# The first group of a fused attention and MLP kernel: another order of loads, casts and row blocks

## The chip, the cores and the metric

The kernel runs on one core of a Trainium2 chip. The metric is device time in microseconds (us). Before the change the median of 10 runs is 310.26 us (309.45 to 311.67). The engines are TensorE (PE: matrix products and, with an identity matrix, transposes), VectorE (DVE), ScalarE (ACT: exp, GELU, copies and casts), GpSimd (POOL: element work[...]) and SyncE (SP), whose queue issues the DMAs.

## The reference

The reference is an attention over pooled keys and values, followed by an MLP with the tanh form of GELU. B = 8 batches, H = 8 heads, S = 576 positions, D = 64, so 4608 rows of 512 columns enter the MLP, whose inner width is 2048. All inputs and the output are float32.

```python
k_p = k.reshape(B, H, Sp, pool, D).mean(axis=3)     # pool = 8, Sp = 72
v_p = v.reshape(B, H, Sp, pool, D).mean(axis=3)
scores = scale * np.matmul(q, k_p.transpose(0, 1, 3, 2))
scores = scores - np.max(scores, axis=-1, keepdims=True)
attn = np.exp(scores)
attn = attn / (np.sum(attn, axis=-1, keepdims=True) + 1e-09)
attn_out = np.matmul(attn, v_p)
x = np.ascontiguousarray(attn_out.transpose(0, 2, 1, 3)).reshape(B * S, H * D)
h = x @ w_in
g = 0.5 * h * (1.0 + np.tanh(c * (h + 0.044715 * h * h * h)))
out = g @ w_out
```

## The kernel before

**Groups.** The rows go through in nine groups of 512. Group g (0 to 7) holds the first 512 positions of batch g; group R (index 8) holds the last 64 positions of all eight batches. The order is 0 to 6, R, 7. A group has four row blocks j of 128 rows.

**Attention of a group.** K and V arrive in one tile `kv` (`load_main`, `load_half`). `pool` sums eight positions in three DVE additions (lines 128 to 130) into `kvb`; for two of V's parts of batch 0 `pool_v_pe` does it with 16 PE products instead (line 136). K is doubled (`dup_k`), transposed and copied by `k_spread` into `kbd`, in which each pair of heads has its own 64 partitions, the others being zero. `spread_v` multiplies V on POOL with a mask (line 148) into `vbd`. q is loaded, cast to bf16 (`cast_q`) and transposed to `qT`. For each row block, `scores` makes four products (line 208; for group R eight products, line 213, half of the rows each, since each 64 rows belong to another batch), `exps` takes the exponential on ACT from PSUM (line 221), `norm` sums, inverts and multiplies (lines 228, 230 and 231) into `eb`, and `eb` is transposed to `eT`: on PE (`e_transpose_pe`, line 240) for group 0, by a transposing DMA (`e_transpose_dma`, line 244) for the others. `values` multiplies with `vbd` (line 267; R line 273) and ACT copies the result to `xT`. Group 0 does this in halves of 256 rows (`values_half`, line 256).

**MLP of a group.** `hidden` (line 297) makes 16 column blocks fo of the first product, each from four partial products ko, and ACT applies GELU (line 299) into `gT`. `output` (line 302) makes the second product, 64 products of 512 columns, and `finish` copies and stores.

**The order.** It is written out by hand. While PE does the products of one group, functions of the next group's attention are called at numbered steps: `at(hooks, s, f, ...)` calls f just before the s-th product. An engine works through its instructions in the order of these calls. Every table (`preload_act_table_set`) is loaded on ACT where the call stands.

**The first group** is apart. Before it there is only a prologue (lines 362 to 460): loads, warm-up products on PE (`warm_up`, line 411), the attention of group 0, and casts of the weights. The weights w_in and w_out come as float32 in four chunks of 1 MB each and are cast to bf16 once (`cast_w_in`, `cast_w_out`, through the helper `copy`, lines 78 and 80). w_in chunk c holds the column blocks fo = 4c to 4c + 3; w_out chunk c holds the same fo of the second product. `mlp_first` goes through (half of the rows, chunk) pairs: steps 0 to 127 are products of the first kind with 256 columns, steps 128 on are products of the second kind, for fo 0 to 11 with the four row blocks inside, and then fo 12 to 15 for each row block.

**Loads and buffers.** All loads stand in SP's queue in program order: K, half tiles, half of q, V and the other half of q of batch 0; the four chunks of w_in; K, half tiles, q and V of batch 1; the four chunks of w_out. The tiles `kv`, `w_in_s` and `w_out_s` share three buffers (pool `kvp`), so batch 1's K waits until batch 0's V was read, and the w_out tiles wait for the casts of w_in. SP also holds the transposing DMAs and the stores.

Of the kernel before, what the change touches and what calls it, by code (L numbers as in the profile page):

```python
# [8 lines left out]
F32 = mybir.dt.float32  # L9
BF16 = mybir.dt.bfloat16  # L10
ALU = mybir.AluOpType
# [8 lines left out]
def kernel(  # L20
# [55 lines left out]
    def copy(eng, out, in_):  # L76
        if eng is nc.scalar:
            eng.copy(out=out, in_=in_)  # L78
        else:
            eng.tensor_copy(out=out, in_=in_)  # L80
# [121 lines left out]
    def scores(g, j):  # L202
        sc = psum.tile([128, 2, MAIN], F32, name="sc", tag="sc", bufs=2)
        qT = st[g]["qT"]
        for pr in range(HP):
            o = sc[:, pr // 2, 2 * Sp * (pr % 2):2 * Sp * (pr % 2) + 2 * Sp]
            if g < B:
                nc.tensor.matmul(out=o, lhsT=qT[:, j, pr, :], rhs=kbd[:, g, pr].rearrange("d hh s -> d (hh s)"),  # L208
                                 start=True, stop=True)
            else:  # L210
                for half in range(2):
                    p0 = 64 * half
                    nc.tensor.matmul(out=o[p0:p0 + 64], lhsT=qT[:, j, pr, p0:p0 + 64],
                                     rhs=kbd[:, 2 * j + half, pr].rearrange("d hh s -> d (hh s)"),
                                     start=True, stop=True)
        st[g][("sc", j)] = sc
# [8 lines left out]
    def norm(g, j, eng):  # L225
        e = st[g][("e", j)]
        den = work.tile([128, H], F32, name="den")
        nc.vector.reduce_sum(out=den, in_=e, axis=AX.X)  # L228
        r = work.tile([128, H], F32, name="r")
        nc.vector.reciprocal(out=r, in_=den)  # L230
        eng.tensor_tensor(out=eb[:, j, 128 * 5 - W:].rearrange("p (h s) -> p h s", s=Sp), in0=e,  # L231
                          in1=r.unsqueeze(2).to_broadcast([128, H, Sp]), op=ALU.mult)
# [16 lines left out]
    def values_half(g, half, engs):  # L249

        for x in range(2):
            xo = psum.tile([128, 2, 256], F32, name="xo", tag="mm", bufs=4)
            for i in range(2):
                pr = 2 * x + i
                for y, (c, n) in enumerate(PARTS[pr]):
                    nc.tensor.matmul(out=xo[:, i, :], lhsT=vbd[:, g, n, :],
                                     rhs=st[g]["eT"][:, 2 * half:2 * half + 2, c, :], start=(y == 0), stop=(y == 1))
            copy(engs[x], st[g]["xT"][:, 2 * x:2 * x + 2, 256 * half:256 * half + 256], xo)
# [77 lines left out]
    def mlp_first(g, hooks):  # L336
# [3 lines left out]
        for half, c in [(0, 0), (0, 1), (0, 2), (0, 3), (1, 0), (1, 1), (1, 2), (1, 3)]:  # L340
            for fo in range(4 * c, 4 * c + 4):
                hidden(g, fo, 256 * half, 256 * half + 256, hook, s)
                s += 4
# [24 lines left out]
    load_q(0, 0, 2, nc.sync)  # L368
    load_main(0, "v", 0, 2, nc.sync)
    load_main(0, "v", 2, 4, nc.sync)  # L370
    load_q(0, 2, 4, nc.sync)
# [10 lines left out]
    def cast_w_in(c, eng):  # L382
        o = 512 * c
        copy(eng, w_in_b[:, :, o:o + 512], w_in_s[c // 2][:, :, 512 * (c % 2):512 * (c % 2) + 512])
# [46 lines left out]
    warm_up(14, "mm")  # L431
    cast_q(0, 0, 2, nc.vector)
    q_transpose_pe(0, 0, nc.vector, "mm")
    q_transpose_pe(0, 1, nc.scalar, "mm")
    warm_up(6, "sc")
    for j in range(2):
        scores(0, j)
        exps(0, j)
    pool(0, 5, 7)
    spread_v(0, nc.gpsimd, (0,))  # L440
    pool_v_pe(0, 7, 9, nc.scalar)
    spread_v(0, nc.gpsimd, (1, 2))
    warm_up(8, "mm")
    norm(0, 0, nc.vector)
    norm(0, 1, nc.vector)
    cast_q(0, 2, 4, nc.scalar)
    e_transpose_pe(0, 0, nc.scalar)
    q_transpose_pe(0, 2, nc.scalar, "mm")
    q_transpose_pe(0, 3, nc.scalar, "mm")
    for j in range(2, 4):  # L450
        scores(0, j)
        exps(0, j)
    nc.scalar.preload_act_table_set(GELU_SET)
    e_transpose_pe(0, 1, nc.vector)
    cast_w_in(0, nc.vector)
    values_half(0, 0, [nc.scalar, nc.vector])
    norm(0, 2, nc.gpsimd)
    cast_w_in(1, nc.vector)
    norm(0, 3, nc.vector)
    cast_w_in(2, nc.gpsimd)  # L460
# [4 lines left out]
    def first_v():  # L465
        cast_w_in(3, nc.vector)
        values_half(0, 1, [nc.scalar, nc.vector])
# [8 lines left out]
    load_main(1, "v", 0, 4, nc.sync)  # L476
    for c in range(4):
        w_out_load(c)
# [20 lines left out]
    at(hooks, 16, first_t, 2)  # L499
    at(hooks, 32, first_t, 3)  # L500
    at(hooks, 42, first_v)
    at(hooks, 66, pool, 1, 0, 4)
    at(hooks, 66, dup_k, 1, 0, 4)
    at(hooks, 66, pool, 1, 4, 5)
    at(hooks, 66, dup_k, 1, 4, 5)
    at(hooks, 80, cast_q, 1, 0, 2, nc.vector)
    at(hooks, 80, cast_q, 1, 2, 4, nc.vector)
# [3 lines left out]
    at(hooks, 96, k_spread, 1, [nc.vector, nc.vector])  # L511
    for j in range(4):
        at(hooks, 104 + 6 * j, q_transpose_pe, 1, j, nc.vector, "sc")
    at(hooks, 122, eT_tile, 1)
    at(hooks, 122, pool, 1, 5, 9)
    at(hooks, 122, spread_v, 1, nc.gpsimd)
    at(hooks, 122, cast_w_out, 0, nc.gpsimd)
    at(hooks, 122, cast_w_out, 1, nc.gpsimd)
# [6 lines left out]
    at(hooks, 141, cast_w_out, 3, nc.scalar)  # L525
# [3 lines left out]
    tail_of_attention(hooks, 1, 186)  # L529
# [75 lines left out]
```

## Time and profile before

| | us |
|---|---|
| median of 10 runs | 310.26 |
| profiled execution | 311.05 |
| its span | 309.3 |
| PE busy (95% of the span) | 294.3 |
| ACT busy (51%) | 158.8 |
| DVE busy (47%) | 145.2 |
| POOL busy (18%) | 56.3 |
| first product with w_in starts | 20.17 |
| first product with w_out starts | 45.27 |
| values of batch 1 start | 61.34 |

The profile is one execution on the chip, and its times start at the beginning of the span. A busy PE isn't PE at its peak[...]. Idle time of another engine costs nothing unless PE waits for that engine in the end. An instruction's wait is put down to what came last.

### The profile page before, as it was taken

Reading aid. Unit: us, or ns where it says so; the run is one execution under the profiler, and the core shown is the slowest. Engines: PE = TensorE matmul, PEld = TensorE weight load, DVE = VectorE, ACT = ScalarE, POOL = GpSimd, SP = SyncE. Lnnn points to the kernel's source line nnn. Section 1 sums busy time; section 2 is a strip of 40 time slices with the busy share of each in tenths; the row PEclk is TensorE's granted clock in tenths of the full one; section 3 lists DMA queues with packets and bytes.
Section 4 is the critical chain, followed back from the end, with each engine's and each line's share of the span. In section 5 each row is a group of like instructions: output and inputs, shape, how many; then the busy total and the mean of one; then the engine's idle time right before and its main releaser. Section 6 shows DMA issues by size and latency. Waiting matters only on the chain.

```text
span 309.3 us, 4581 instructions
## 1 busy us (share of the span) xinstructions
PE 294.3 (95%) x1738; PEld 153.8 (50%) x1738; DVE 145.2 (47%) x237; ACT 158.8 (51%) x242; POOL 56.3 (18%) x71
## 2 busy tenths in 40 slices
PE   8969919999999999999999999999999999999996
PEld 8748904444544454445444544444444544544444
DVE  6877774162551755176435734483448200720012
ACT  1477734376806671667257626752674257625600
POOL 3323071022130312032203310340024000100000
PEclk9999986999999999999999999999999999999999
DMA  8999982899169937993899289437983810261012
GB/s 243 359 387 342 386 277 43 244 353 222 28 147 287 281 97 138 316 259 85 140 317 275 60 151 316 125 75 162 323 193 77 167 47 2 53 135 36 0 64 72
DMA packets 73221, 56.32 MB, mean 182 GB/s; under 512 B 45808, under 2 KB 55408, under 8 KB 73200
## 3 DMA queue, kind: packets, MB, share of 16 engines
q1 hardware_dynamic: 73056, 55.98, 65.6%
q8 instruction: 13, 0.21, 0.3%
q14 instruction: 8, 0.07, 0.1%
q10 hardware_dynamic: 144, 0.07, 0.1%
HBM read 36.70 MB, written 9.44 MB: 149 GB/s over the span
## 4 chain that ended last, share of the span: by engine, by line
PE 86%; DMA 4%; DVE 3%; POOL 2%; SPq 1%; ACT 1%; issue 1%; DVEq 0%; POOLq 0%
PE mm L297 40%; PE mm L302 37%; PE xo L267 4%; DMA q_sb<-in_q_dram 3%; PE sc L208 2%; DMA eT<-eb 1%; PE mm L330 1%; DVE den L228 1%; POOL w_out_b L80 1%; POOL vbd L148 1%; POOL eb L231 1%; SPq L98 1%; PE xo L273 1%; DVE kv L128 0%; DVE w_in_b L80 0%
## 5 line engine op out<-in xcount | busy, mean ns | idle before, releaser
L302 PE MATMUL mm<-w_out_b,gT 128*128 128x512 bf16 x560 | 131.1, 384 | 6.3 <-POOL w_out_b L80 6.3
L297 PE MATMUL mm<-xT,w_in_b 128*128 128x512 bf16 (+1 forms) x640 | 127.6, 358 | 0.8 <-ACT xT L78 0.8
L299 ACT ACTIVATE gT<-mm 128x512 bf16<-128x512 f32 (+1 forms) x160 | 88.7, 555 | 48.1 <-PE mm L297 46.8
L297 PEld LDWEIGHTS <-w_in_b 128*128 128x128 bf16 x640 | 62.3, 98 | 62.8 <-issue 0.6
L302 PEld LDWEIGHTS <-gT 128*128 128x128 bf16 x560 | 54.1, 99 | 66.6 <-issue 8.7
L80 DVE COPY osb<-mm 128x512 f32<-128x512 f32 (+2 forms) x37 | 24.4, 659 | 70.1 <-PE mm L302 68.0
L228 DVE TENSOR_REDUCE den<-e 128x8 f32<-128x576 f32 x36 | 26.5, 737 | 46.3 <-ACT e L221 46.3
L78 ACT CAST xT<-xo 128x1024 bf16<-128x1024 f32 (+1 forms) x18 | 16.6, 967 | 57.4 <-PE xo L267 48.9
L148 POOL TENSOR_TENSOR vbd<-kvb,vmask 128x256 bf16<-128x256 bf16 (+2 forms) x40 | 20.3, 531 | 118.7 <-DVE kvb L130 118.4
L128 DVE TENSOR_TENSOR kv<-kv 128x1024 f32<-128x1024 f32 (+3 forms) x19 | 22.0, 1160 | 24.1 <-DMA kv<-in_v_dram 22.7
L221 ACT ACTIVATE e<-sc 128x576 f32<-128x576 f32 x36 | 22.3, 649 | 17.9 <-PE sc L208 11.7
L231 DVE TENSOR_TENSOR eb<-e,r 128x576 bf16<-128x576 f32 x28 | 27.5, 982 | 1.2 <-DVE r L230 0.2
L231 POOL TENSOR_TENSOR eb<-e,r 128x576 bf16<-128x576 f32 x8 | 10.0, 1251 | 79.9 <-ACT e L221 46.0
L80 POOL CAST q_b<-q_sb 128x2048 bf16<-128x2048 f32 x6 | 14.0, 2332 | 13.6 <-DMA q_sb<-in_q_dram 13.6
L208 PEld LDWEIGHTS <-qT 128*128 128x128 bf16 x128 | 10.4, 101 | 8.0 <-issue 1.1
L208 PE MATMUL sc<-kbd,qT 128*128 128x144 bf16 x128 | 13.6, 232 | 0.5 <-ACT qT L78 0.5
L267 PE MATMUL xo<-eT,vbd 128*128 128x512 bf16 x56 | 13.2, 379 | 0.0
L129 DVE TENSOR_TENSOR kv<-kv 128x512 f32<-128x512 f32 (+3 forms) x19 | 12.3, 649 | 0.6
L411 PE MATMUL warm<-identb 128*128 128x128 bf16 x116 | 9.9, 258 | 1.4 <-POOL vmask L399 1.4
L490 ACT ACT_TABLE_LOAD x8 | 10.3, 1283 | 0.1
L411 PEld LDWEIGHTS <-identb 128*128 128x128 bf16 x116 | 9.1, 120 | 1.5 <-POOL vmask L399 1.4
L80 DVE COPY kbd<-kTd 64x288 bf16<-64x288 bf16 x12 | 5.3, 440 | 8.5 <-DMA kTd<-kvb 8.4
(54 smaller groups left out, 102.6 us busy)
## 6 DMA issues: line engine op xcount, KB each, us to landing
out_dram<-osb SPq DMA_DIRECT2D x31, 256.0 KB, 6.4
kv<-in_k_dram SPq DMA_DIRECT2D x7, 1024.0 KB, 6.8
q_sb<-in_q_dram SPq DMA_DIRECT2D x7, 1024.0 KB, 5.8
kv<-in_v_dram SPq DMA_DIRECT2D x7, 1024.0 KB, 9.4
w_in_s<-in_moe_w_in_dram SPq DMA_DIRECT2D x4, 1024.0 KB, 12.5
w_out_s<-in_moe_w_out_dram SPq DMA_DIRECT2D x4, 1024.0 KB, 13.9
out_dram<-osb SPq DMA_DIRECT2D x9, 128.0 KB, 2.3
kv<-in_k_dram SPq DMA_DIRECT2D x2, 512.0 KB, 4.0
```

Source lines behind the costliest of these rows:

```text
L80: eng.tensor_copy(out=out, in_=in_)
L128: add(out=t[:, :, 0:4, :], in0=t[:, :, 0:4, :], in1=t[:, :, 4:8, :], op=ALU.add)
L148: eng.tensor_tensor(out=vbd[p0:128, b, n0:n1, :].rearrange("p (c r) (hh d) -> p c (r hh) d", c=max(m, 1), d=D), in0=kvb[p0:128, 4 + c0:4 + ...
L208: nc.tensor.matmul(out=o, lhsT=qT[:, j, pr, :], rhs=kbd[:, g, pr].rearrange("d hh s -> d (hh s)"), start=True, stop=True)
L221: nc.scalar.activation(out=e.rearrange("p (x h) s -> p x (h s)", x=2), in_=sc[:, :, 0:4 * Sp], func=ACT.Exp, scale=1.0 / 64.0)
L228: nc.vector.reduce_sum(out=den, in_=e, axis=AX.X)
L231: eng.tensor_tensor(out=eb[:, j, 128 * 5 - W:].rearrange("p (h s) -> p h s", s=Sp), in0=e, in1=r.unsqueeze(2).to_broadcast([128, H, Sp]), ...
L267: nc.tensor.matmul(out=xo[:, i, :], lhsT=vbd[:, g, n, :], rhs=eT[:, :, c, :], start=(x == 0), stop=(x == 1))
L297: nc.tensor.matmul(out=hp[:, 0:c1 - c0], lhsT=w_in_b[:, ko, fo * 128:(fo + 1) * 128], rhs=st[g]["xT"][:, ko, c0:c1], start=(ko == 0), stop ...
L299: nc.scalar.activation(out=gT[:, fo, c0:c1], in_=hp[:, 0:c1 - c0], func=ACT.Gelu_apprx_tanh)
L302: nc.tensor.matmul(out=o, lhsT=gT[:, fo, r * 128:(r + 1) * 128], rhs=w_out_b[:, fo, :], start=(fo == 0), stop=(fo == FO - 1))
L411: nc.tensor.matmul(out=warm[:, 0:128], lhsT=identb, rhs=identb, start=True, stop=True)
```

## The change

The change has these parts.

- q of batch 0 comes in one load, ahead of V. Its cast is split over DVE (block 0), ACT (block 1) and POOL (blocks 2 and 3). All four blocks are transposed, scored and exponentiated one after the other, and ACT's table for GELU is loaded after the last exp; then V is pooled and spread, and blocks 0 and 1 are normalised.
- w_in chunk 0 is cast half by POOL and half by ACT, chunks 1 and 3 by POOL, chunk 2 by DVE inside `first_v`, which is now called at step 32. Blocks 2 and 3 are both normalised on DVE and transposed at steps 12 and 24. Both copies of the first half's values are on ACT.
- `mlp_first` takes the second half of the rows through chunk 0 before the first half through chunk 3.
- Batch 1: K, the half tiles and q are loaded first, then w_out chunks 0 and 1, half of V, chunk 2, the other half of V, chunk 3. V is pooled and spread at step 160 (before: 122). q is cast at step 100 (before: 80). w_out chunk 0 is cast by DVE at step 124 (before: POOL), chunk 3 by ACT at step 156.
- Group R: each of a row block's eight score products becomes two, with only the 64 partitions of one head, 64 rows and 72 columns; even heads go to one PSUM bank and odd heads to the other, and `norm` puts them back in order when it writes `eb`.

```diff
-            else:
-                for half in range(2):
-                    p0 = 64 * half
-                    nc.tensor.matmul(out=o[p0:p0 + 64], lhsT=qT[:, j, pr, p0:p0 + 64],
-                                     rhs=kbd[:, 2 * j + half, pr].rearrange("d hh s -> d (hh s)"),
-                                     start=True, stop=True)
+            for hh in range(2):
+                for p0 in (0, 64):
+                    h0 = 64 * hh
+                    nc.tensor.matmul(out=sc[p0:p0 + 64, hh, Sp * pr:Sp * pr + Sp],
+                                     lhsT=qT[h0:h0 + 64, j, pr, p0:p0 + 64],
+                                     rhs=kbd[h0:h0 + 64, 2 * j + p0 // 64, pr, hh], start=True, stop=True)
...
+            eng.tensor_tensor(out=o.rearrange("p (pr hh s) -> p hh pr s", hh=2, s=Sp),
+                              in0=e.rearrange("p (hh pr) s -> p hh pr s", hh=2),
...
-        for half, c in [(0, 0), (0, 1), (0, 2), (0, 3), (1, 0), (1, 1), (1, 2), (1, 3)]:
+        for half, c in [(0, 0), (0, 1), (0, 2), (1, 0), (0, 3), (1, 1), (1, 2), (1, 3)]:
...
-    load_q(0, 0, 2, nc.sync)
+    load_q(0, 0, 4, nc.sync)
     load_main(0, "v", 0, 2, nc.sync)
     load_main(0, "v", 2, 4, nc.sync)
-    load_q(0, 2, 4, nc.sync)
...
-    warm_up(14, "mm")
-    cast_q(0, 0, 2, nc.vector)
+    warm_up(12, "mm")
+    cast_q(0, 0, 1, nc.vector)
+    cast_q(0, 1, 2, nc.scalar)
+    cast_q(0, 2, 4, nc.gpsimd)
     q_transpose_pe(0, 0, nc.vector, "mm")
     q_transpose_pe(0, 1, nc.scalar, "mm")
-    warm_up(6, "sc")
...
+    q_transpose_pe(0, 2, nc.vector, "mm")
+    scores(0, 0)
+    exps(0, 0)
+    scores(0, 1)
     q_transpose_pe(0, 3, nc.scalar, "mm")
-    for j in range(2, 4):
+    exps(0, 1)
+    for j in (2, 3):
         scores(0, j)
         exps(0, j)
     nc.scalar.preload_act_table_set(GELU_SET)
+    pool(0, 5, 7)
+    spread_v(0, nc.gpsimd, (0,))
+    spread_v(0, nc.gpsimd, (1,))
+    pool_v_pe(0, 7, 9, nc.scalar)
+    spread_v(0, nc.gpsimd, (2,))
+    norm(0, 0, nc.vector)
+    norm(0, 1, nc.vector)
+    cast_w_in(0, nc.gpsimd, 0, 2)
+    e_transpose_pe(0, 0, nc.scalar)
+    cast_w_in(0, nc.scalar, 2, 4)
+    warm_up(8, "mm")
     e_transpose_pe(0, 1, nc.vector)
-    cast_w_in(0, nc.vector)
-    values_half(0, 0, [nc.scalar, nc.vector])
-    norm(0, 2, nc.gpsimd)
-    cast_w_in(1, nc.vector)
+    values_half(0, 0, 0, nc.scalar)
+    values_half(0, 0, 1, nc.scalar)
+    norm(0, 2, nc.vector)
+    cast_w_in(1, nc.gpsimd)
     norm(0, 3, nc.vector)
-    cast_w_in(2, nc.gpsimd)
+    cast_w_in(3, nc.gpsimd)
...
     def first_v():
-        cast_w_in(3, nc.vector)
-        values_half(0, 1, [nc.scalar, nc.vector])
+        values_half(0, 1, 0, nc.vector)
+        values_half(0, 1, 1, nc.scalar)
+        cast_w_in(2, nc.vector)
...
     load_q(1, 0, 4, nc.sync)
-    load_main(1, "v", 0, 4, nc.sync)
-    for c in range(4):
-        w_out_load(c)
+    w_out_load(0)
+    w_out_load(1)
+    load_main(1, "v", 0, 2, nc.sync)
+    w_out_load(2)
+    load_main(1, "v", 2, 4, nc.sync)
+    w_out_load(3)
...
-    at(hooks, 16, first_t, 2)
-    at(hooks, 32, first_t, 3)
-    at(hooks, 42, first_v)
+    at(hooks, 12, first_t, 2)
+    at(hooks, 24, first_t, 3)
+    at(hooks, 32, first_v)
...
-    at(hooks, 80, cast_q, 1, 0, 2, nc.vector)
-    at(hooks, 80, cast_q, 1, 2, 4, nc.vector)
...
+    at(hooks, 100, cast_q, 1, 0, 2, nc.vector)
+    at(hooks, 100, cast_q, 1, 2, 4, nc.vector)
     for j in range(4):
-        at(hooks, 104 + 6 * j, q_transpose_pe, 1, j, nc.vector, "sc")
-    at(hooks, 122, eT_tile, 1)
-    at(hooks, 122, pool, 1, 5, 9)
-    at(hooks, 122, spread_v, 1, nc.gpsimd)
-    at(hooks, 122, cast_w_out, 0, nc.gpsimd)
-    at(hooks, 122, cast_w_out, 1, nc.gpsimd)
+        at(hooks, 111 + 4 * j, q_transpose_pe, 1, j, nc.vector, "sc")
+    at(hooks, 124, eT_tile, 1)
+    at(hooks, 124, cast_w_out, 0, nc.vector)
+    at(hooks, 124, cast_w_out, 1, nc.gpsimd)
...
-    at(hooks, 141, cast_w_out, 3, nc.scalar)
+    at(hooks, 156, cast_w_out, 3, nc.scalar)
+    for i in range(2):
+        at(hooks, 160, pool, 1, 5 + 2 * i, 7 + 2 * i)
+        at(hooks, 160, spread_v, 1, nc.gpsimd, (0, 1) if i == 0 else (2,))
...
-    tail_of_attention(hooks, 1, 186)
+    tail_of_attention(hooks, 1, 187)
```

## The prediction

> **What bounds the kernel now.** I read the slices first (40 of 7.73 us; busy tenths of TensorE, PE, and its granted clock). PE is at nine tenths or more except in slices 1, 3 and 6 and the last, and only in 6 and 7 (38.7 to 54.1 us) does its clock drop.
>
> ```profile
> PE   8969919999999999999999999999999999999996
> PEclk9999986999999999999999999999999999999999
> ```
>
> So the place is the first group of rows; the groups after it leave PE hardly a gap. The table of stretches shows how deep the hole is (columns: stretch, length, busy us of PE, PE weight loads, VectorE (DVE), ScalarE (ACT), GpSimd (POOL), PE clock, DMA share, GB/s):
>
> ```profile
> 38.00:40.00 2.00, 0.97 (x13) 0.78 (x11) 1.97 (x3) 1.36 (x3) 0.00 (x0) 1.00 1.08 392
> 40.00:42.00 2.00, 0.00 (x0) 0.00 (x0) 1.17 (x3) 1.89 (x3) 1.26 (x3) 1.00 1.03 380
> 42.00:44.00 2.00, 0.00 (x0) 0.00 (x0) 1.86 (x4) 0.00 (x0) 2.00 (x3) 1.00 0.80 295
> 44.00:46.00 2.00, 0.73 (x2) 0.25 (x2) 1.76 (x3) 0.00 (x0) 2.00 (x2) 0.59 0.68 132
> 46.00:48.00 2.00, 2.00 (x6) 0.76 (x5) 0.00 (x0) 0.00 (x0) 1.58 (x1) 0.50 0.42 82
> ```
>
> The chain that ended last says what PE waited for (start, length, piece):
>
> ```profile
> 37.86 0.42 DVE qT L80
> 38.28 1.15 DVE kv L128
> ...
> 40.17 0.44 DVE kvb L130
> ...
> 40.74 2.11 POOL vbd L148 x4
> 42.85 2.38 POOL w_out_b L80
> 45.23 0.04 issue
> 45.27 3.57 PE mm L302 x8
> 48.84 0.48 PE sc L208 x4
> 49.32 1.71 PE mm L302 x4
> 51.03 0.38 PE sc L208 x4
> 51.41 9.93 PE mm L302 x46
> ```
>
> The second product's first weights are cast on POOL behind the pooling and spreading of batch 1's V. PE's last w_in product ends at 38.97, and the next starts at 45.27: 6.3 us lost. Twelve L302 products then take 3.57 + 1.71 = 5.28 us, where the next 46 take 0.216 each; with the two score sets (0.86 against 2 x 0.25) the cold clock costs 2.69 + 0.36 = 3.05 us. The waits name a smaller loss, the wait of group 0's third row block for its normalisation on POOL:
>
> ```profile
> PE tp L240 <- POOL eb L231: 1.1, 1, 1.1
> ```
>
> [...] 6.29 us idle, then clock 0.50 until about 51 us. [...] The trace has only 128x64 tiles, with 0.42 us of idle weight load before each set; no 64x64. [...] the same POOL normalisation takes 1.95 us beside VectorE's casts and 1.15 us later.
>
> **The change part by part.** I follow the new order to the end of the first group.
>
> *Up to the first w_in product.* q is one load, and V follows it. Before, q's first half landed at 8.6 us (issued 3.06, 5.5 to landing) and V's first half at 10.0, both 512 KB; exchanging V's first half for q's second, q lands at 10.0 to 10.3. Three casts run side by side (DVE half of its 0.67, ACT about 0.6, POOL about 1.1), done by 11.4. Transposes (0.35 a block), copies (0.42 DVE, 0.59 ACT), four score sets and four exps (0.6 each) alternate, since two score buffers let set 2 wait for exp 0; ACT ends at 15.25, loads its table (1.28) until 16.5. V's products on PE (2.0) come behind the scores, 14.4 to 16.4. DVE pools V (1.4) and normalises blocks 0 and 1 (1.85 each), 12.3 to 17.4. ACT: V's copy 0.27, e copy 0.69, half of w_in chunk 0 (about 1.0), to 18.55; POOL: spread and other half of chunk 0, to 19.0. Second e block 17.45, copy to 18.4, values 0.9, ACT copies to 20.1. Before, the first w_in product began at 20.17. I take 19.95 as equivalent start (its first two products can start ahead of the second copy): **-0.2**, between -1.2 (ACT faster) and +1.5 (q late).
>
> *The w_in products.* The 1.1 wait goes: block 2 is normalised on DVE by 20.2, the hook comes at 21.4: **-1.1**. Chunk 1 moves from DVE (1.2) to POOL (2.42 beside DVE), behind chunk 0 and the landing at about 19.7, done 22.1; needed at 19.95 + 16 x 0.1095 + 0.28 = 21.98: **+0.2** (0 to 1). Chunk 2 moves from POOL, cast long ahead, to DVE inside the values step that stands directly before the products that read it. DVE takes values in order, so xT's copy (0.69) and then the cast (1.22) run after the first half of the values; only 0.43 of values on PE hides them: 0.69 + 1.22 - 0.43 = **+1.5**. Behind that cast wait only batch 1's K sums, whose data land at 28.7. Chunk 3 on POOL starts at its landing, 25.0, ends 27.5, needed at about 28: hidden; uncovered it costs what it is late. The reordering (the second half of the rows goes through chunk 0 before chunk 3 is touched) adds no product: 128 of 256 columns stay. The 8 warm-up products that go lie in waits for casts, off the path. The casts of batch 1's q move behind K's spreading: 0.55 transposes, 0.62 spread, 0.76 cast against 15 x 0.1095 + 0.36 of PE work: **+0.1**.
>
> *The second product.* w_out chunk 0 now stands in SP's queue ahead of V, 1 MB less; at the 385 GB/s of these stretches 2.7 us earlier, about 35.1 instead of 37.8. The SP waits on its way: K of batch 1 waits for V's products (16.4 instead of 14.0), but by the GB/s of the stretches only 5.0 of the 7.6 MB issued had moved then, so the engines have work; w_out 0 waits for POOL's cast of chunk 1 (22.1), with 2.7 MB outstanding; w_out 2 for the casts of chunks 2 and 3 (27.5), with 3.5. All 15.2 MB still move, without a gap; V's two halves, last issued behind w_out 0 to 1 and 2, land near 39 and 43. Chunk 0's cast is on DVE, behind the fourth qT copy: 0.42 + 1.22 after the last transposes, PE has 1.05 of products and scores: **+0.7** with the handover. So the second product starts at 38.97 - 0.2 - 1.1 + 0.2 + 1.5 + 0.1 + 0.7 = 40.17: 5.1 before 45.27. [...] the clock stays: **-3.05**. Chunk 1 (POOL, landed 37.8, done 40.2) is needed at 44.1, chunk 2 (ACT after the exps, 43.9 to 45.8) at 47.5, chunk 3 (about 45.8 to 47.9) at 51: hidden with 1.7 us or more.
>
> *V of batch 1.* Its pooling (two of 1.4) moves behind the four normalisations on DVE: the last GELU at 39.9, ACT's table 1.28 and an exp 0.6 let them begin at 41.8, 4 x 1.87 to 49.3, sums to 52.1, POOL's last spread to 53.1; block 3's transposing DMA, 2.6, to about 52. values come at 40.17 + 59 x 0.216 + 0.5 = 53.4. Cover 0.3 us; [...] **+0.2** (0 to 1.5). The next batch's loads take the buffer that w_out's first two chunks leave, free from 40.2, but go out on SP behind these DMAs, 3.4 us later against PE than before; its K had 3.6 us to spare (spread at 75.07, scores at 78.65): 0, or 0.5 when the landing slips.
>
> *Group R's scores.* 8 products of 128x64 by 144 (0.37 a set) become 16 of 64x64 by 72. Fully overlapped they would take half (-0.7 over four sets), one by one at the present 46 ns 0.74 (+1.5). PE has no gap at the scores, so it counts in full: **+0.4**. The normalisation's other order keeps 576 elements: 0.76 to 1.0 as before.
>
> Sum: -5.1 - 3.05 + 0.2 + 0.4 = -7.55. The profiled execution took 311.05 for a span of 309.3; it lies 0.79 above the median of 310.26. Span 301.75, that execution 303.5, median **302.7 us**.
>
> **Rivals.**
> *The first group becomes bound by its own chain* (13 in 100): q later, or w_in chunks 1 and 3 late on POOL, whose casts vary from 1.9 to 2.49. For it: three POOL casts in a row and the stall at chunk 2. Against: POOL had 5.7 us idle there. Each us passes on; 1.3 to 4.3 gives 304 to 307.
> *w_out comes no earlier* (4): the queue loses K's later issue of 2.4 us and gains nothing. Then chunk 0 lands at 40.2, is cast at 41.4: +1.3, 304. Against: the engines were saturated (392, 380 GB/s).
> *V late for the values* (7): 1 to 2.5 us of wait, 303.7 to 305.2.
> *Slower: R's quarter products run one by one with full latency* (4). [...] It decides from (7.95 + 1.48)/64 = 147 ns a product. Against: the 128x64 products overlap at 46 ns[...].
>
> **How the numbers follow.** The forecast as written has 65 in 100 and 301 to 304.5 as its own range; better than that 4 (chunk 2's wait hidden, quarters overlapping: down to 299.4). The range 299.8 to 307 takes in the forecast, the first three rivals nearly whole, and leaves out R's. That several rivals together eat the gain has 3: 2 within 0.2% (about what a measurement of this kernel can tell from no change) and 1 slower. Faster is 65 + 4 + 13 + 4 + 7 = 93, same 2, slower 4 + 1 = 5.
>
> **What would show it.** Right: slices 6 and 7 at full clock, no POOL w_out_b wait above 1 us, the first L302 product near 40.2, values of batch 1 near 53.4; a PE wait of about 1.5 us for DVE's w_in_b before the third chunk; R's sets near 0.47 us. Wrong: a first w_in product after 22, idle time of PE above 3 us anywhere before 53, or R's sets above 1 us.

## The result, and the profile after

The changed kernel has a median of 305.88 us in nine runs (302.75 to 306.60), the kernel before beside it 310.30 (309.45 to 311.67). The ratio is 0.984, with a 95% interval of 0.982 to 0.986. It is faster by 4.4 us; the forecast was 302.7.

The median hides something. The times of the changed kernel lie in two groups with nothing between them. Of 15 executions of it in this study (eleven here and four in the first experiment) five took 302.75 to 303.48 us, with PE's mean granted clock at 1.000 of full speed, and ten took 305.45 to 306.60, with 0.994. I call them the lower and the upper level. The kernel before shows no such gap: its runs fill 309.2 to 311.7 us, with a clock of 0.983 to 0.989. The profile of the changed kernel shows an execution of the lower level: 302.79 us, span 301.1. So the forecast has to be held against two things: its steps against this profile, and its number against a median that belongs to the upper level. Lines have moved: L297 is now L305, L302 is L310, L267 is L275, L231 is L235, and L213 is L215.

The slices show that the hole of before is gone. PE's tenths stay below nine in slices 1 to 4, and the clock is never lowered:

```profile
PE   8777999999999999999999999999999999999996
PEclk9999999999999999999999999999999999999999
```

The chain that ended last (start, length, piece) gives the dates that the forecast named:

```profile
26.51 1.35 DVE w_in_b L80
...
27.91 7.16 PE mm L305 x64
...
39.83 1.26 DVE w_out_b L80
...
41.14 1.90 PE mm L310 x8
...
43.29 0.86 PE mm L310 x4
...
44.40 10.14 PE mm L310 x47
54.55 1.73 PE xo L275 x8
```

The second product starts at 41.14 instead of 45.27, and its first twelve products take 1.90 + 0.86 = 2.76 us where they took 5.28. The values of batch 1 come at 54.55 instead of 61.34. The remaining waits of PE for a cast of weights in the first 62 us (total, times, longest) are two:

```profile
PE mm L305 <- DVE w_in_b L80: 1.6, 1, 1.6
PE mm L310 <- DVE w_out_b L80: 0.7, 1, 0.7
```

One thing in the timeline of VectorE and GpSimd (start, length, instruction) was not forecast. The normalisation of row block 2 takes 2.48 us, where before and after it the same instruction takes 0.76 to 1.01:

```profile
18.29 3.07 POOL L80 CAST w_in_b<-w_in_s 128x1024 bf16<-128x1024 f32 x2
19.48 2.48 DVE L235 TENSOR_TENSOR eb<-e,r 128x576 bf16<-128x576 f32 x1
...
24.88 1.90 POOL L80 CAST w_in_b<-w_in_s 128x2048 bf16<-128x2048 f32 x1 [3.52 <-DMA w_in_s<-in_moe_w_in_dram]
...
26.51 1.34 DVE L80 CAST w_in_b<-w_in_s 128x2048 bf16<-128x2048 f32 x1
```

POOL's two casts (half of chunk 0, then chunk 1) end at 18.29 + 3.07 = 21.36, 1.88 after the start of the normalisation, and this takes 1.72 longer than 0.76 and ends 0.60 after POOL: it looks like a wait for POOL. The second of these casts starts at 19.46, 0.05 after its load has landed and only 0.02 ahead of the normalisation. Further down, VectorE's cast of chunk 2 meets POOL's cast of chunk 3. POOL ends at 26.78, VectorE 1.07 later, at 27.85. Here only 0.27 us of POOL's cast were left when VectorE began, and VectorE's took 1.34, little more than the 1.22 of the profile of before, where such a cast of VectorE's (18.20) has no POOL instruction beside it.

### The profile page after: what moved, and what is told of

The parts are those of the page before. It is cut to its first block, busy times and chain, and to the rows that moved or that the text cites. A ratio compares the mean times of both kernels' runs of the same rounds, so it can differ in the third digit from the quotient of the medians.

```text
span 301.1 us, 4636 instructions
## 1 busy us (share of the span) xinstructions
PE 290.2 (96%) x1762; PEld 151.5 (50%) x1762; DVE 147.0 (49%) x240; ACT 159.3 (53%) x243; POOL 56.1 (19%) x72
## 4 chain that ended last, share of the span: by engine, by line
PE 90%; DVE 5%; issue 3%; POOL 1%; POOLq 0%
PE mm L305 40%; PE mm L310 40%; PE xo L275 4%; PE sc L208 2%; DVE eb L235 2%; PE mm L338 1%; DVE den L230 1%; PE xo L281 1%; DVE w_in_b L80 0%; PE tp L193 0%; POOL q_b L80 0%; DVE w_out_b L80 0%; PE sc L215 0%; PE tp L249 0%; DVE eT L80 0%
## 5 line engine op out<-in xcount | busy, mean ns | idle before, releaser
L305 PE MATMUL mm<-xT,w_in_b 128*128 128x512 bf16 (+1 forms) x640 | 127.8, 358 | 2.0 <-DVE w_in_b L80 1.6
L310 PE MATMUL mm<-w_out_b,gT 128*128 128x512 bf16 x560 | 128.6, 379 | 0.7 <-DVE w_out_b L80 0.7
L305 PEld LDWEIGHTS <-w_in_b 128*128 128x128 bf16 x640 | 62.3, 98 | 64.2 <-DVE w_in_b L80 1.9
L310 PEld LDWEIGHTS <-gT 128*128 128x128 bf16 x560 | 53.4, 98 | 59.7 <-DVE w_out_b L80 1.0
L148 POOL TENSOR_TENSOR vbd<-kvb,vmask 128x256 bf16<-128x256 bf16 (+2 forms) x40 | 21.2, 554 | 111.6 <-DVE kvb L130 109.9
L128 DVE TENSOR_TENSOR kv<-kv 128x1024 f32<-128x1024 f32 (+3 forms) x20 | 22.7, 1135 | 28.8 <-DMA kv<-in_v_dram 27.1
L235 DVE TENSOR_TENSOR eb<-e,r 128x576 bf16<-128x576 f32 x26 | 26.2, 1007 | 0.9
L235 POOL TENSOR_TENSOR eb<-e,r 128x576 bf16<-128x576 f32 x6 | 6.9, 1151 | 62.0 <-ACT e L223 34.7
L80 POOL CAST q_b<-q_sb 128x2048 bf16<-128x2048 f32 (+1 forms) x7 | 15.3, 2183 | 9.6 <-DMA q_sb<-in_q_dram 9.6
L275 PE MATMUL xo<-eT,vbd 128*128 128x512 bf16 x56 | 13.2, 379 | 0.0
L418 PE MATMUL warm<-identb 128*128 128x128 bf16 x108 | 8.9, 254 | 1.4 <-POOL vmask L406 1.4
```

Of the source, the lines that this page charges most:

```text
L128: add(out=t[:, :, 0:4, :], in0=t[:, :, 0:4, :], in1=t[:, :, 4:8, :], op=ALU.add)
L148: eng.tensor_tensor(out=vbd[p0:128, b, n0:n1, :].rearrange("p (c r) (hh d) -> p c (r hh) d", c=max(m, 1), d=D), in0=kvb[p0:128, 4 + c0:4 + ...
L235: eng.tensor_tensor(out=o.rearrange("p (h s) -> p h s", s=Sp), in0=e, in1=r.unsqueeze(2).to_broadcast([128, H, Sp]), op=ALU.mult)
L275: nc.tensor.matmul(out=xo[:, i, :], lhsT=vbd[:, g, n, :], rhs=eT[:, :, c, :], start=(x == 0), stop=(x == 1))
L305: nc.tensor.matmul(out=hp[:, 0:c1 - c0], lhsT=w_in_b[:, ko, fo * 128:(fo + 1) * 128], rhs=st[g]["xT"][:, ko, c0:c1], start=(ko == 0), stop ...
L310: nc.tensor.matmul(out=o, lhsT=gT[:, fo, r * 128:(r + 1) * 128], rhs=w_out_b[:, fo, :], start=(fo == 0), stop=(fo == FO - 1))
```

## The experiments

All kernels ran against the kernel before on the same chip, whose median was 309.97 to 310.86. Where a number of microseconds is compared across them, each is taken from the profile of the kernel named.

### The changed kernel again

Nothing is edited. The question was whether the two levels belong to the kernel, and what the upper one looks like.

> The changed kernel once more, for its second level. Nine runs gave 302.75 and 303.48 us at a mean PE clock of 1.000 and seven between 305.45 and 306.6 at 0.994. 0.006 of 304 us at full rate missing is 3.65 us at half rate[...]. Theory A (sparse prologue): the clock falls in a window between 10 and 20 us, where PE is busy 0.45, 0.73, 0.76, 0.41 us of each us from 10 to 14. Theory B (the new stall): it falls after the 1.6 us that PE waits for w_in chunk 2 at 26.3. A profile at 0.994 should show the clock row below 9 in slice 2 or 3 under A, in slice 4 or 5 under B.

Measured: 304.42 us median, runs of 302.78, 303.21, 305.64 and 306.03, ratio 0.980 (0.975 to 0.985). Both levels are there again, and the profile now shows the upper one (305.64 us, span 303.9). Its timeline, all engines:

```profile
19.15 0.76 DVE L235 TENSOR_TENSOR eb<-e,r 128x576 bf16<-128x576 f32 x1
19.20 2.46 POOL L80 CAST w_in_b<-w_in_s 128x2048 bf16<-128x2048 f32 x1 [0.22 <-DMA w_in_s<-in_moe_w_in_dram]
...
24.63 1.90 POOL L80 CAST w_in_b<-w_in_s 128x2048 bf16<-128x2048 f32 x1 [2.97 <-DMA w_in_s<-in_moe_w_in_dram]
25.19 2.41 DVE L80 CAST w_in_b<-w_in_s 128x2048 bf16<-128x2048 f32 x1
27.66 8.73 PE L305 MATMUL mm<-xT,w_in_b 128*128 128x256 bf16 x64 [2.67 <-DVE w_in_b L80]
...
37.44 3.05 DVE L80 CAST q_b<-q_sb 128x1024 bf16<-128x1024 f32 x2
39.74 0.40 PE L193 MATMUL tp<-identb,q_b 128*128 128x128 bf16 x4 [1.25 <-DVE q_b L80]
```

Read it against the lower level. The normalisation of block 2 came first this time (0.76 us), so PE did not wait early, and VectorE reached the cast of chunk 2 at 25.19 instead of 26.51. That was too early: POOL's cast of chunk 3 had started at 24.63, and VectorE's cast took 2.41, ending at 27.60, again 1.07 after POOL's. Yet the third chunk's products start at 27.66, which is earlier than the 27.91 of the lower level. The loss comes after that. PE stood still for 2.67 us in one piece, and then its clock falls, as the clock row (slice 4 is 22.8 to 30.4 us, where Theory B had it) and the stretches (the column before the last two) show:

```profile
PEclk9998999999999999999999999999999999999999
...
26.00:28.00 2.00, 0.34 (x2) 0.28 (x3) 1.60 (x1) 0.00 (x0) 0.52 (x1) 0.88 1.09 289
28.00:30.00 2.00, 2.00 (x12) 1.38 (x10) 1.86 (x2) 0.77 (x2) 0.00 (x0) 0.50 1.09 343
```

The 64 products take 8.73 instead of 7.16: +1.57. Being late, the casts of batch 1's q then fall into POOL's cast of w_out chunk 1 (37.24 to 39.14), take 3.05 instead of 1.29, and PE waits 1.25 for them. The sum, -0.25 + 1.57 + 1.25 = 2.57, is the difference of the second product's start, 43.77 - 41.14 = 2.63, and of the spans, 303.9 - 301.1 = 2.8. So a VectorE cast that takes 2.41 beside POOL's, the clock of 0.50 that follows it, and q's casts of 3.05 beside POOL's next one make the upper level (I call such an overlap, in which one of the two instructions takes longer, a collision); what the prologue does up to 20 us is the same within 0.35 us.

Who comes first at 19.5 us is a close thing. POOL's cast of chunk 1 starts 0.05 after its load has landed: at 19.46 in the lower level, where VectorE comes at 19.48, and at 19.20 in the upper one, where VectorE has come at 19.15. Three profiles of kernels that follow fit this: POOL is first by 0.04 in the one with products without use, at full clock (1.000), and VectorE by 0.09 and 0.15 in those with R's scores as before and with only the first group's part, both with a lowered clock behind chunk 2 (0.59 and 0.54 in 28 to 30).

### The cast of chunk 2 ahead of the values

```diff
     def first_v():
+        cast_w_in(2, nc.vector)
         values_half(0, 1, 0, nc.vector)
         values_half(0, 1, 1, nc.scalar)
-        cast_w_in(2, nc.vector)
```

> Chunk 2's cast moves ahead of the values in the same step, DVE is free there from 25.1. Both theories: the wait of 1.6 us for DVE w_in_b falls below 0.3, so 1.4 to 1.6 us less at each level, about 301.3 and 304.4. Theory A: two levels stay, median near 304.4. Theory B: the lower clock goes, all runs near 301.3.

Measured: 300.01 us median, runs of 299.88, 299.92, 300.10 and 302.75, all at a clock of 1.00; ratio 0.968 (0.963 to 0.973). The chain after it:

```profile
24.41 0.87 PE xo L264 x8
25.29 7.13 PE mm L305 x64
```

The cast runs from 23.98 to 25.20 (1.22 us) while PE still has products and values to do. It starts ahead of POOL's chunk 3 (24.86), and here POOL's cast is the one that takes longer (2.09 instead of 1.90); PE doesn't wait for that. PE goes from the values to the third chunk's products without a wait. The second product starts at 38.37, 2.77 earlier than in the lower level of the changed kernel: block 2 is normalised ahead of POOL here (0.76), so the 0.96 us that its lateness cost, reckoned below, are gone together with the 1.61; together they are 2.57 of the 2.77. Theory B had all runs near 301.3. The clock is as it said, three runs are 1.3 lower, most of it the early waits that are gone, and what made the one run of 302.75 is not shown.

### Group R's scores as before

```diff
-            for hh in range(2):
-                for p0 in (0, 64):
-                    h0 = 64 * hh
-                    nc.tensor.matmul(out=sc[p0:p0 + 64, hh, Sp * pr:Sp * pr + Sp], ...
+            else:
+                for half in range(2):
+                    p0 = 64 * half
+                    nc.tensor.matmul(out=o[p0:p0 + 64], lhsT=qT[:, j, pr, p0:p0 + 64], ...
```

The order in `norm` goes back with it; all else is the changed kernel.

> Group R's scores and normalisation as before, all else changed. The stage from R's predecessor to R's first product took 32.20 us before and 30.93 after. If the quarter products did that: 4 x (0.37 - 0.25) = 0.5 us of product time and the 0.6 us wait for eT come back, 1.1 to 1.3 slower than the changed kernel at each level, 304.0 and 307.1. If my forecast of a cost of 0.4 was right: 0.4 faster.

Measured: 304.68 us median, runs of 302.98, 303.00, 306.35 and 306.39; ratio 0.981 (0.975 to 0.987). Both levels stay. Their middles, 302.99 and 306.37, lie 0.2 and 0.5 above those of the changed kernel (302.79 and 305.88). The timelines give the size. A set of scores in the kernel before, and in the changed kernel:

```profile
230.51 0.44 PE L213 MATMUL sc<-kbd,qT 128*64 128x144 bf16 x8
```

```profile
223.51 0.32 PE L215 MATMUL sc<-kbd,qT 64*64 64x72 bf16 x16
```

The next product starts at 230.89 and at 223.77, so a set costs 0.38 and now 0.26, 16 ns for each of its sixteen products. Four sets save 0.48. The forecast of 1.1 to 1.3 had also put back a wait of 0.6 for a transposing DMA, and this wait did not come back.

### Only batch 1's part

The kernel before, with only the loads of batch 1 and w_out, the casts of q and w_out, and V's pooling as in the change (the first group and group R as before).

> Only the part on batch 1 and w_out is made: load order, casts of w_out, late V, q's cast; prologue, w_in casts, order of chunks and R stay as before. My sum: 6.3 of wait becomes 0.7, the clock's 3.05 goes: 8.65 less, 0.2 given back at the values, median 301.9. Theory A: the old prologue keeps the clock, one level near 301.9, below the changed kernel's median. If the first group's part is needed for the gain (values of batch 1 late, w_out late): 304 or more. The rival that the new prologue matters: 308 or more.

Measured: 304.99 us median (304.20 to 306.24), ratio 0.982 (0.979 to 0.985). This cannot be told from the whole change, and it is 3.1 above the forecast of 301.9. It has a collision of its own: POOL's cast of w_out chunk 1 starts at 38.91, VectorE's of chunk 0 at 39.23, and the latter takes 2.65 (1.34 in the profile of the changed kernel). In the table of waits:

```profile
PE mm L302 <- DVE w_out_b L80: 2.0, 1, 2.0
```

The forecast had 0.7 for this wait, which explains 1.3 of the miss. In the profiled execution the first w_in product also starts at 21.10, 0.93 later than in the profile before. The rest is open. The single level that was forecast isn't there either: three runs have a clock of 1.000, and the fourth, of 306.24 us, has 0.994.

### Only the first group's part

The counterpart: the changed kernel with everything of batch 1 put back (V whole before w_out, both first w_out casts on POOL behind V's spreading at step 122).

> Only the first group's part and group R's part: the loads of batch 1 and of w_out, q's casts, V's pooling and the w_out casts stand where the kernel before has them. If the gain comes from w_out chunk 0 being there before V (cast on VectorE), this is no faster than the kernel before by more than group R's 0.5 and the first group's few tenths: 309 to 311, with PE's clock at 0.5 after the second product starts and a wait of PE for POOL's w_out_b of more than 5 us. If the first group's part carries a share of its own (the wait for block 2's normalisation, earlier reading of batch 0's V), it is 306 to 308.5.

Measured: 310.96 us median in 14 runs (309.99 to 313.36) against 310.05 in 19; ratio 1.0034 (1.0011 to 1.0056). The first group's part alone is slower by 0.9 us at the median, though it contains group R's gain of 0.5. It has two levels of its own: seven runs at a clock of 0.989 with a median of 310.36, about the time of the kernel before, and seven at 0.982 to 0.984 with 312.25. The profile is of the latter (312.19). Two lines of its waits say why it gains nothing:

```profile
PE mm L310 <- POOL w_out_b L80: 6.3, 1, 6.3
PE mm L305 <- DVE w_in_b L80: 2.8, 1, 2.8
```

The wait that bounds the kernel before is whole, and the collision at chunk 2 (2.50 for VectorE's cast) has come on top; in the profile the 64 products after it take 8.83 us, at a clock of 0.54 in 28 to 30 and 0.60 in 30 to 32.

### POOL's casts in pieces

In the upper level VectorE's cast of chunk 2 began 0.56 us after POOL's of 1.90 and ended 1.07 after it, and took 2.41, where it takes 1.34 in the lower level. My reading of these times is that VectorE waits for the rest of POOL's instruction. Then a shorter POOL instruction must shorten the wait. POOL's three weight casts are cut into four pieces each; the rest is the changed kernel.

```diff
-    cast_w_in(1, nc.gpsimd)
+    for f in range(4):
+        cast_w_in(1, nc.gpsimd, f, f + 1)
     norm(0, 3, nc.vector)
-    cast_w_in(3, nc.gpsimd)
+    for f in range(4):
+        cast_w_in(3, nc.gpsimd, f, f + 1)
...
-    at(hooks, 124, cast_w_out, 1, nc.gpsimd)
+    for f in range(4):
+        at(hooks, 124, cast_w_out, 1, nc.gpsimd, f, f + 1)
```

> POOL's casts of w_in chunks 1 and 3 and of w_out chunk 1 are cut into four pieces of 512 columns each; everything else is the changed kernel. [...] (from 1.3 to 2.4 us, when a 1.90 us cast of POOL starts just ahead of it), then VectorE has to wait for one piece at most: its cast takes 1.9 us or less, PE waits 2.1 us or less for it, the clock is 1.000 in every run, and the time is 302 to 303.5 in all of them. If the cast is slow for another reason (the writes of the loads that land meanwhile, or PSUM), it still takes 2.4 us in the slow executions, and the runs keep two levels, 302.8 to 303.5 and 305.5 to 306.5.

Measured: 302.12 us median (301.88 to 302.55, four runs, clock 0.998 to 1.000), ratio 0.974 (0.971 to 0.977). The timeline:

```profile
24.68 3.28 POOL L80 CAST w_in_b<-w_in_s 128x512 bf16<-128x512 f32 x4 [2.02 <-DMA w_in_s<-in_moe_w_in_dram]
25.43 1.50 DVE L80 CAST w_in_b<-w_in_s 128x2048 bf16<-128x2048 f32 x1
```

VectorE starts its cast 0.75 us after POOL (0.56 in the upper level, where it took 2.41), and now takes 1.50. None of the four runs is on the upper level. The pieces make POOL slower in all (3.28 for 1.90 here), which costs nothing because no one waits for it.

### Both edits

The cast of chunk 2 first, and POOL's casts in pieces.

> Both edits together: the cast of w_in chunk 2 ahead of the values on VectorE, and POOL's casts in four pieces. [...] all runs lie at 299.5 to 300.3 with a clock of 1.000. If pieces cost POOL more than they spare VectorE (a longer chunk 1, needed at about 22), it is 300.3 to 301.5. If something else makes the slower run, one run in four still lies near 302.7.

Measured: 300.32 us median (299.82 to 300.82, five runs), ratio 0.968 (0.966 to 0.970). The same as with the cast first alone. No run lies near 302.7, but five runs are too few to say that such runs are gone. The next two kernels start from this one.

### The loads of batch 1 in the old order

```diff
-    w_out_load(0)
-    w_out_load(1)
-    load_main(1, "v", 0, 2, nc.sync)
-    w_out_load(2)
-    load_main(1, "v", 2, 4, nc.sync)
-    w_out_load(3)
+    load_main(1, "v", 0, 4, nc.sync)
+    for c in range(4):
+        w_out_load(c)
```

> The kernel with both edits (cast of w_in chunk 2 first, POOL's casts in pieces), and in it only the order of batch 1's loads is that of before: the whole of V, and then w_out chunks 0 to 3. All casts, pooling and hooks stay. If the order of the loads is what brings chunk 0 in time, as the prediction's step on the second product says, chunk 0 lands 2.7 us later, near 37.8 instead of 35.1, VectorE's cast starts there instead of 37.1, the second product starts about 0.8 later (39.1), and chunks 1 to 3, each later by 1.4 to 2.7 us, begin to hold PE: 301 to 303. If the place and the engine of the cast carry the gain alone, it stays within 0.3 of the kernel with both edits: 300.0 to 300.6.

Measured: 300.43 us median (300.21 to 300.67), ratio 0.967 (0.965 to 0.970), against 300.32. The chain:

```profile
37.49 1.24 DVE w_out_b L80
...
38.77 1.90 PE mm L310 x8
```

Chunk 0 lands at 37.47, and at 35.07 with both edits; the prediction's working has 37.8 and 35.1. VectorE, which has been waiting for it for 0.50, casts it then. The second product starts at 38.77 instead of 38.35. So the place in SP's queue, 2.4 us by these landings, is worth 0.4 on the path in the profile, and nothing that the times show. What the change needed was the place of the cast, not that of the load.

### Chunk 0 cast on POOL

The kernel before this one, with the engine of one cast exchanged (`cast_w_out, 0, nc.gpsimd`), still ahead of V's pooling and spreading.

> The previous kernel, and besides w_out chunk 0 cast on POOL, in one piece of 1.90 us, ahead of chunk 1 and of V's spreading (V's pooling and spreading stay at step 160). If what gated the second product before was only that the cast stood behind V on POOL, the engine costs the difference of the two casts, 1.90 for 1.22, less the time in which VectorE is still busy with qT: 0.3 to 0.7 more than the previous kernel, and 0.5 to 1.5 more again if chunk 1, now behind it on POOL, comes late for fo 4. If VectorE as the engine is what matters, PE waits over 3 us for POOL's cast, its clock falls, and the time is above 305.

Measured: 301.47 us median, runs of 301.05, 301.08, 301.85 and 303.02; ratio 0.972 (0.968 to 0.975). The profile is that of the last. Its chain:

```profile
37.74 1.90 POOL w_out_b L80
...
39.69 3.29 PE mm L310 x8
```

The lowest two are 0.6 above the previous kernel, about what 1.90 for 1.24 costs. In the profiled run PE waited 2.00 us, its clock was 0.50 in 40 to 42, and eight products took 3.29 for 1.90. So the engine costs some 0.6 in itself, and more in the two executions with a lowered clock (301.85 us at 0.998 and 303.02 at 0.994, where the other two have 0.999 and 1.000).

### Products without use in PE's wait

To part the wait from the clock, 28 products of 128 columns are put behind the values of the second half, where PE waits for chunk 2.

```diff
         cast_w_in(2, nc.vector)
+        warm_up(28, "mm")
```

> 28 products without use (about 1.6 us, 0.057 each) stand behind the values of the second half of the rows, in the time in which PE waits for the cast of w_in chunk 2. If the lower clock of the slower executions comes from PE's wait of 2.7 us there, the clock is 1.000 in every run, and the slower level comes down by the 1.57 us of slow products: 302.8 to 303.3 and about 304.3 (the longer waits themselves stay). If the clock falls for another reason, 0.994 and 305.5 to 306.5 remain in about half of the runs.

Measured: 302.63 us median (302.57 to 302.78), ratio 0.976 (0.973 to 0.978), clock 0.999 to 1.000 in all four. The upper level is not there, but the profile is of an execution in which the normalisation was held up (2.46) and the cast was not (1.35), so this run alone doesn't show the case in question. My figure of about 304.3 for it was wrong too: the third chunk's products start no later in the upper level than in the lower, so without the lowered clock there is nothing left to be slower by.

### A pause on POOL, and the pause with those products

To have VectorE's normalisation go first on purpose, a memset of 0.52 us without use is put between POOL's casts of chunk 0 and chunk 1. Nothing waits for it.

```diff
+    idle = consts.tile([128, 512], F32, name="idle")
...
     norm(0, 2, nc.vector)
+    nc.gpsimd.memset(idle, 0.0)
     cast_w_in(1, nc.gpsimd)
```

> The changed kernel with one POOL instruction without use, a memset of 128x512 float32 (about 0.5 us), between POOL's casts of w_in chunk 0 and chunk 1. Nothing on the path waits for it. [...] The memset lets VectorE go first in every execution: its normalisation takes 0.76, no early wait, VectorE reaches the cast of chunk 2 at about 25.3, in the middle of POOL's chunk 3 (24.7 to 26.7), the cast takes 2.4, PE waits 2.6 to 2.8, the clock falls: every run at 305.4 to 306.5 with a clock of 0.994. Rival, the levels come from the landing of loads or another source: both levels stay, 302.8 to 303.5 and 305.5 to 306.5.

Measured: 305.65 us median, runs of 305.64, 305.67, 305.75 and 303.00; ratio 0.983 (0.979 to 0.988). In the profile (of the upper level) the normalisation takes 0.76, there is no early wait, VectorE's cast of chunk 2 starts at 25.54 and takes 2.02, PE waits 2.29 and its 64 products take 8.83. The profile is as forecast, but one run of four stayed on the lower level, so what VectorE does at 19.5 us doesn't decide alone. Nor do the times show that the pause changed anything: three of four are on the upper level here, and ten of fifteen without it. The rival, that landings make the levels, is not excluded: POOL's cast of chunk 3 starts at its landing (24.59 here), and without the pause so does that of chunk 1.

With the memset and the 28 products together:

> The same memset, and besides the 28 products without use in PE's wait for the cast of chunk 2. If the lower clock of the upper level comes from PE's wait of 2.7 us, it is now 1.000 although VectorE's cast still takes 2.4, the third chunk's products start at about 27.7 (as without the memset, 27.9), the later collision on q's cast goes too, since the products end 1.6 earlier, and every run lies at 302.2 to 303.2. If the clock falls for another reason, 0.994 and 305.4 to 306.5 stay.

Measured: 302.69 us median (302.54 to 302.90), ratio 0.976 (0.974 to 0.977), clock 0.999 to 1.000. Now the profile has the case that was missing (all lines are one further on here, by that of the memset's tile):

```profile
25.61 2.39 DVE L81 CAST w_in_b<-w_in_s 128x2048 bf16<-128x2048 f32 x1
28.05 7.16 PE L306 MATMUL mm<-xT,w_in_b 128*128 128x256 bf16 x64 [1.09 <-DVE w_in_b L81]
```

The cast is as slow as in the upper level, but PE has had 1.73 us of products without use in the wait, the 64 products take 7.16, q's cast meets nothing (1.29), and the time is that of the lower level. So the lowered clock, with the collision that its loss of time brings about, accounts for the difference between the levels.

## Why the prediction was right, and where it was not

The sign, the mechanism of the main gain and the range (299.8 to 307.0) held. The median is 3.2 us above the forecast. It lies outside the 301 to 304.5 that the prediction gave as the forecast's own range; the wide range holds it by the room left for the rivals. Point by point:

**The start of the w_in products.** Forecast 19.95, as an equivalent start. The first product came at 19.97 (19.63 in the second profile), but the third waited for the second copy of the values, so the equivalent start is about 20.2 (19.9). Right within 0.3.

**"The 1.1 wait goes."** This failed in the profile of the lower level. The prediction had block 2 normalised on DVE by 20.2; it was 21.96, because the normalisation, beside POOL's casts, took 2.48 for 0.76. Counted from start to start, PE's first twelve products took 22.02 - 19.97 = 2.05 for 1.31 of work, and the next twelve 24.11 - 22.31 = 1.80 for 1.31. Of the 1.23 lost, 0.27 is the wait for the second copy, which the second profile has too (21.21 - 19.63 = 1.58); the other 0.96 is the late normalisation. Before, sixteen products took 23.16 - 20.17 = 2.99 for 1.74: 1.25 lost. So 0.3 was gained of the 1.1, and what is left of the wait is in two pieces. In the upper level all of it went.

**"Chunk 1 ... +0.2."** It was 0: POOL was done at 21.36, ahead of 21.98.

**Chunk 2, "+1.5", and "Chunk 3 on POOL ... hidden".** This is the step that put the median above the forecast. The wait was forecast at 1.5 and is 1.6 in the lower level, so the term looks right there. But it was made up of a VectorE cast priced at 1.22, and the POOL cast of chunk 3 beside it was judged only by whether PE would wait for it. It starts at its landing (forecast 25.0, measured 24.6 to 25.0), that is where VectorE's cast begins, and VectorE loses the rest of POOL's instruction less 0.15: in the lower level 0.27 was left and the cast took 1.34 for 1.22, in the upper one 1.34 was left and it took 2.41. The prediction's own figures put the two side by side: 19.95, 32 products of 0.1095, two blocks of transposes of 0.28, 0.43 of values and a copy of 0.69 make 25.1 for the start of VectorE's cast. It gave POOL's cast 2.5 (25.0 to 27.5) and left VectorE's at 1.22. The profiles agree closely. VectorE's cast of 128x2048 ended 1.07 us after POOL's in the lower level and the upper level, and the same figure comes out of three others: with only the first group (26.59, 27.66), only batch 1 (40.81, 41.88) and the pause on POOL (26.49, 27.56). The prediction had an allowance of 0.2 at V's sums, of which two take 0.72 for 0.42 and 0.58 for 0.29 beside POOL's spreading while PE waits for nothing, and none for the two casts that the change puts at the same time.

**"The clock stays: -3.05", for a pause of 0.7.** Right for that pause: it was 0.73, the clock is 1.00 in 38 to 48, and the first twelve second products and two score sets got their 3 us back. That so short a pause leaves the clock alone was the author's estimate; the profile of before has a clock of 0.50 behind a pause of 6.29 us and of 1.00 behind one of 1.1. And it looked at one pause only. The other one, at chunk 2, grows to 2.67 when the casts collide, and then costs 1.57 of clock, and 1.25 at q's cast. Measured, the clock was lowered behind waits of 2.00 (chunk 0 cast on POOL, 0.50 in 40 to 42), 2.29 (the pause on POOL, 0.58 in 28 to 30) and 2.67 us (the upper level, 0.50 in 28 to 30), and not behind one of 2.04 in the profiled execution of only batch 1 (1.00 in 42 to 44), though another run of that kernel has a mean clock of 0.994. The traces don't show which of these a given execution gets.

**The q casts, "+0.1".** Right in the lower level, 1.25 in the upper one.

**The second product "0.7 with the handover", and its start at 40.17.** The handover was 0.73. The start was 41.14, late by 0.97, which is the sum of the misses above: +0.3 (the start), +0.8 (block 2), -0.2 (chunk 1), +0.1 (chunk 2). That chunk 0 "now stands ahead of V, 2.7 us earlier" was given as its ground. The old order of loads shows that this was no condition: the load was early enough behind V as well, within 0.4. What had held the second product back was that its cast stood behind V's pooling and spreading on POOL. Every kernel here with the gain has both the cast ahead of V and V at step 160, so which of these two moves is needed is not shown.

**V of batch 1, "+0.2".** It was 0. The last spread ended at 54.10, 0.28 ahead of the values' first product in the timeline (54.38), and PE did not wait: V's pooling at step 160 is hidden, with about the cover of 0.3 that was forecast.

**Group R, "+0.4 (-0.7 to +1.5)".** The middle of the bounds was the wrong choice: the sets cost 0.26 for 0.38, -0.48 in all, near the -0.7 at which the prediction put full overlap. The serial rival, which needed 147 ns a product to decide, fell: it is 16 ns from start to start. The 196 ns that the profile shows for one product run to a modelled end, so the starts alone are counted.

**The sum.** The forecast for the profiled execution was 303.5, and it took 302.79. That is closer than its parts: at batch 1's values it stood at 54.55, 1.15 later than forecast. From there on it was 1.8 shorter than forecast (301.1 - 54.55 = 246.55 for 301.75 - 53.4 = 248.35). The scores of group R are 0.88 of that (forecast +0.4, measured -0.48). Some 0.8 lie in the same stage: from the start of the w_in products ahead of R to the start of R's it is 32.20 us before and 30.93 after, 1.27 less, of which the scores explain 0.48. There the kernel before has PE wait 0.6 us for a transposing DMA, and the changed kernel doesn't. With R's scores put back this wait is absent too, and with only batch 1's part it is there (0.5), so it doesn't come from R's scores; why that DMA lands earlier is open. Two misses cancelled here, so that this execution came out near its forecast is luck, and the median lies 3.1 us above this profile because two thirds of the executions are on the other level.

**The rivals.** "The first group becomes bound by its own chain", by w_in chunks late on POOL, 304 to 307, had 13 in 100. The median is where it put it and its place is right, but its mechanism is not: chunks 1 and 3 were in time, and it was VectorE's cast of chunk 2 that came late, at 2.41 beside POOL's for 1.22. W_out no earlier, V late, and R serial did not happen. For the first group the prediction's terms (-0.2, -1.1, +0.2, +1.5, +0.1) add up to a loss of 0.5, and its part alone did gain nothing (310.96 for 310.05); the 5.9 of batch 1's part (310.86 to 304.99) is the gain. As the change has it, the first group's part adds nothing to that which can be measured (305.88 and 304.42 for the whole), and 5.0, R's scores included, when chunk 2's cast leaves the place that the change gave it (300.01).

## What to carry to other kernels

When a change spreads casts over VectorE and GpSimd, draw their intervals side by side, with the landing of each source as the start, and charge the second one the rest of the first. This held here for casts (2.41 for 1.22) and for the two-input normalisation (2.48 for 0.76); a sum of 0.75 us on VectorE, and a copy from PSUM of 0.69, ran beside POOL's casts without loss in the upper level's profile. A cast hidden by the usual test, that PE doesn't wait for it, doubled another cast for which PE did. Put a cast that PE needs ahead of the work that it would follow, or cut the other engine's instruction into pieces. Add up the pauses of PE one by one with their worst length, since pauses of 2.00, 2.29 and 2.67 us were paid twice here, and try the parts of a change alone: one part carried the whole gain, and another was worth something only after an edit of one line.

## What was not expected of the hardware

- Products without use, 1.73 us of them in PE's wait for chunk 2, brought the runs with the pause from 305.65 to 302.69, though the cast that PE waits for stayed as slow (2.39).
- In the changed kernel the smoother start is the slower one. When VectorE's normalisation starts ahead of POOL's cast (19.15 and 19.20), PE has no early wait, and VectorE arrives in time for the worse collision at 25 us (2.41 for the cast). When it starts behind (19.48 and 19.46), PE loses 0.96 us in two short pieces, at which the clock did not fall (1.00).
- POOL's cast of chunk 3 (128x2048) in four pieces takes 3.28 us beside VectorE's cast, and 2.29 with VectorE's cast first, where one piece takes 1.90.
- Sixteen 64x64 products of 72 columns take 0.26 us from start to start of what surrounds them, 16 ns each, where eight of 128x64 by 144 columns took 0.38 us.
